# Batch 0 of a windowed attention with a squared-ReLU layer behind it: begun in two groups of 256 tokens, with a smaller masking bias and a new order of the first steps

## The chip, the core and the metric

One core of a Trainium2 chip runs the whole kernel. It has five engines with instruction streams of their own: TensorE (PE, with its weight loads as PEld), VectorE (DVE), ScalarE (ACT), GpSimd (POOL) and SyncE (SP); SP, ACT and POOL issue DMAs, each on a queue of its own. The metric is the device time of one execution in microseconds (us), as the median of several.

## The reference

Attention with four sink tokens and a window of 128, then a two-layer network with a squared ReLU on the result:

```
scores = q @ k.T / sqrt(64);  keep = (key < 4) | (0 <= query - key < 128)
x = (softmax(where(keep, scores, -1e9)) @ v)   # 4 batches, 8 heads, 768 tokens, 64 wide
x = x.transpose(0, 2, 1, 3).reshape(3072, 512)
out = relu(x @ w_in) ** 2 @ w_out              # w_in 512 x 2048, w_out 2048 x 512
```

## The kernel before

All work is cut into numbered steps (`op`, on about 990 places), each for one engine. A table, `ORDER`, lists the steps in the order in which they are recorded, with a letter for the engine that takes the step (p PE, d DVE, a ACT, g POOL) and the choice of a bank; each engine executes its own steps in that order and waits by semaphores for what they need. `DUMMIES` says how many dummy matmuls PE executes ahead of a step (`warm`, line 185, and the warm-up of line 1368, which works on `tri`).

A batch of 768 tokens goes through attention in blocks of 256 tokens (s = 0, 1, 2), and through layer 1 (with w_in) and layer 2 (with w_out) in pieces. For batch 0 the start is this:

- **Loads.** SP loads q and k of the first 512 tokens in fp32 into `qr` (line 351), a pair of heads at a time, 256 KB each, four tokens side by side in a partition. POOL's queue loads v (line 381), w_in in four quarters (line 308), then q and k of the last 256 tokens and of later batches, cast to bf16 on the way (`qn`, line 372), and w_out (line 316). ACT's queue loads four rows of v per head (`vs_in`, line 424), which POOL spreads into `vs` (line 554, "vs products").
- **Transposes.** A cast (line 194 on DVE, 192 on ACT) regroups `qr` into bf16 `qs`; PE transposes it into PSUM (`pt`, line 507); an unload copies it to `qkT` (lines 194, 192).
- **Attention of a block.** Scores of a head pair go to PSUM (`ps`, line 613). In block 0 the mask is added on PE ahead of them, as two matmuls of the identity with `sg`, which holds the bias (line 606). ACT takes the exponential (line 634) into `expm`; in blocks 1 and 2 a mask follows on DVE (line 646) or POOL (line 218). PE multiplies with v (`po`, line 682, "values"); DVE takes a reciprocal and normalizes (lines 698 and 699, "norm") into `xn_sb`. PE transposes that (`px`, line 731, "bridge"), and a copy (line 194 or 192) puts it into `xT`.
- **Layer 1.** A piece is 16 matmuls of 256 columns, a quarter of w_in with a block of 256 tokens (`pm`, line 763); DVE or ACT takes the ReLU and the square. A quarter of w_in has to have landed.

Batch 0 is read in groups of tokens, 512 and 256:

```
GROUPS[0] = [(0, 4), (512, 2)]          # first token, number of blocks of 128
for m in range(NP):                      # NP = 4 pairs of heads
    for ti in (1, 0):                    # k, then q
        load_qk(0, m, ti, 0, 1)
```

The four pairs of heads of the first group come one after the other: cast k, cast q, four transposes each, two unloads, then the pair's scores. The bias is built on POOL (`build_bias`): two selects over four blocks of 128 columns, a copy of them to a second half, and there a memset of the four sink rows.

## Time and profile before

| what | value |
|---|---|
| median of 3 runs | 209.63 us (209.41 to 209.71) |
| the profiled execution: span from its first to its last instruction | 208.6 us |
| PE busy in it | 199.8 us (96%) |
| DVE, ACT, POOL busy | 178.4, 133.0, 98.2 us |
| DMA, software queue (POOL's) | 12.59 MB, 79.6% of 16 engines' span |
| DMA, hardware queue (SP's) | 13.01 MB, 27.0% |

The profile gives no time for the profiled execution other than its span; the runs' median lies 1.0 us above it. In a row of a timeline stand the start in us, the duration in us, the engine, the line of the code, the operation and its tiles, and how many instructions the row merges; in brackets the idle time before the first of them and what ended it. Matmuls are pipelined, so that the starts of a row's neighbours say how long it keeps PE; its duration holds the last matmul's way through the array. In a table of windows each engine has its busy us, with the number of instructions in parentheses; DMA share is the mean over 16 engines and can be above 1 where packets overlap. SPq, ACTq and POOLq are DMA issues.

### The profile page before, as it was taken

What the parts mean: (1) busy time and instruction counts of PE and PEld (TensorE: products, weight loads), DVE (VectorE), ACT (ScalarE), POOL (GpSimd) and SP (SyncE); (2) the same over time, 40 slices, a digit from 0 to 9 for tenths busy, and PEclk for the clock granted to TensorE, in tenths of its full rate; (3) what the DMA queues carried; (4) which work ended last, traced back from release to release, by engine and by line L of the source; (5) the groups of instructions that cost most, each with busy time, mean ns of one, the idle gap of its engine ahead of it and who ended that gap; (6) DMA issues with size and microseconds to landing.
All of it is one profiled execution on the core that took longest, in us unless ns stands there. A gap on an engine that the chain in (4) does not pass through costs nothing.

```text
span 208.6 us, 6015 instructions
## 1 busy us (share of the span) xinstructions
PE 199.8 (96%) x2498; PEld 176.1 (84%) x2500; DVE 178.4 (86%) x342; ACT 133.0 (64%) x208; POOL 98.2 (47%) x138
## 2 busy tenths in 40 slices
PE   7789899999899999999999999999999999999993
PEld 7548796679778889989878988998889999999893
DVE  5757566996989998999998788999989998998853
ACT  2595728548988168899888448989871452584110
POOL 7988164999489936999423628000280000000000
PEclk9999999999999999999999999999999999999999
DMA  5999999999989999999998996901023220200205
GB/s 150 280 185 204 178 193 214 170 155 188 121 55 135 146 142 210 126 167 155 140 149 216 95 129 172 155 3 25 3 50 123 57 80 24 104 0 0 100 4 201
DMA packets 93994, 26.10 MB, mean 125 GB/s; under 512 B 86800, under 2 KB 91408, under 8 KB 93968
## 3 DMA queue, kind: packets, MB, share of 16 engines
q0 software_dynamic: 69248, 12.59, 79.6%
q1 hardware_dynamic: 24536, 13.01, 27.0%
q8 instruction: 19, 0.31, 0.6%
q10 hardware_dynamic: 184, 0.14, 0.2%
q14 instruction: 7, 0.06, 0.1%
HBM read 27.30 MB, written 6.29 MB: 161 GB/s over the span
## 4 chain that ended last, share of the span: by engine, by line
PE 65%; POOL 12%; DVE 9%; DMA 6%; ACT 3%; issue 2%; POOLq 0%; ACTq 0%
PE py L1238 25%; PE pm L891 25%; DMA w_in_sb<-in_moe_w_in_dram 6%; PE pm L763 4%; PE ps L613 4%; POOL v L381 3%; PE po L682 3%; POOL qn L372 3%; POOL vs L554 2%; PE py L1099 2%; ACT expm L634 1%; POOL expm L218 1%; PE pt L507 1%; DVE sg L1212 1%; POOL w_in_sb L308 1%
## 5 line engine op out<-in xcount | busy, mean ns | idle before, releaser
L634 ACT ACTIVATE expm<-ps 128x1024 bf16<-128x1024 f32 (+1 forms) x48 | 43.9, 951 | 9.4 <-PE ps L613 7.5
L218 POOL TENSOR_SCALAR_AFFINE_SELECT expm<-expm 128x512 bf16<-128x512 bf16 x34 | 25.4, 782 | 43.8 <-DVE xn_sb L699 19.5
L941 DVE CUSTOM_DVE_ANT_0 r<-pm,t 128x512 bf16<-128x512 f32 x54 | 36.1, 685 | 1.6 <-PE pm L891 1.1
L1238 PEld LDWEIGHTS <-gT_sb 128*128 128x128 bf16 x320 | 30.4, 98 | 4.5 <-issue 0.8
L891 PEld LDWEIGHTS <-w_in_sb 128*128 128x128 bf16 x384 | 32.4, 114 | 1.7 <-issue 1.5
L192 ACT ACTIVATE t<-pm 128x512 f32<-128x512 f32 x42 | 24.7, 600 | 13.5 <-PE pm L891 12.7
L891 PEld LDWEIGHTS <-wi 128*128 128x128 bf16 x288 | 24.7, 114 | 0.8 <-issue 0.7
L1238 PEld LDWEIGHTS <-sg 128*128 128x128 bf16 x240 | 22.4, 98 | 3.2 <-DVE sg L1212 0.3
L192 ACT ACTIVATE osb<-py 128x256 f32<-128x256 f32 (+1 forms) x36 | 14.1, 398 | 15.7 <-PE py L1238 15.0
L763 PE MATMUL pm<-xT,w_in_sb 128*128 128x256 bf16 x192 | 22.5, 273 | 1.0 <-DMA w_in_sb<-in_moe_w_in_dram 1.0
L763 PEld LDWEIGHTS <-w_in_sb 128*128 128x128 bf16 x192 | 20.5, 114 | 1.9 <-DMA w_in_sb<-in_moe_w_in_dram 1.2
L891 PE MATMUL pm<-xs,wi 128*128 128x256 bf16 (+1 forms) x192 | 21.6, 246 | 0.0
L891 PE MATMUL pm<-xs,w_in_sb 128*128 128x256 bf16 (+1 forms) x192 | 21.5, 246 | 0.0
L1238 PE MATMUL py<-wt,gT_sb 128*128 128x256 bf16 x160 | 20.7, 273 | 0.2
L1238 PE MATMUL py<-wt,sg 128*128 128x256 bf16 x160 | 20.8, 273 | 0.0
L1238 PE MATMUL py<-w_out_sb,gT_sb 128*128 128x256 bf16 x160 | 20.4, 273 | 0.0
L914 ACT ACTIVATE gT_sb<-r 128x1024 bf16<-128x1024 bf16 x17 | 18.0, 1056 | 1.8 <-DVE r L941 1.6
L682 PE MATMUL po<-v,expm 128*128 128x65 bf16 x352 | 17.9, 193 | 0.3 <-ACT expm L634 0.3
L682 PEld LDWEIGHTS <-expm 128*128 128x128 bf16 x352 | 16.7, 97 | 1.7 <-ACT expm L634 0.5
L699 DVE TENSOR_TENSOR xn_sb<-po,rc 128x512 bf16<-128x512 f32 (+1 forms) x28 | 17.2, 615 | 1.0
L1252 DVE TENSOR_TENSOR osb<-py,osb 128x256 f32<-128x256 f32 x30 | 12.1, 418 | 4.7 <-PE py L1238 4.6
L613 PE MATMUL ps<-qkT 64*128 64x128 bf16 (+1 forms) x256 | 14.3, 238 | 0.8 <-ACT expm L634 0.6
(109 smaller groups left out, 383.3 us busy)
## 6 DMA issues: line engine op xcount, KB each, us to landing
out_dram<-osb SPq DMA_DIRECT2D x11, 512.0 KB, 4.9
v<-in_v_dram POOLq DMA_DIRECT2D x24, 128.0 KB, 6.8
qn<-in_k_dram POOLq DMA_DIRECT2D x20, 128.0 KB, 6.5
qn<-in_q_dram POOLq DMA_DIRECT2D x20, 128.0 KB, 6.4
w_in_sb<-in_moe_w_in_dram POOLq DMA_DIRECT2D x4, 512.0 KB, 10.5
w_out_sb<-in_moe_w_out_dram POOLq DMA_DIRECT2D x4, 512.0 KB, 10.9
qr<-in_k_dram SPq DMA_DIRECT2D x4, 256.0 KB, 5.6
qr<-in_q_dram SPq DMA_DIRECT2D x4, 256.0 KB, 5.2
```

Of the source, the lines that this page charges most:

```text
L192: return nc.scalar.activation(out=dst, in_=src, func=AF.Copy)
L218: nc.gpsimd.affine_select(out=e_tile, in_=e_tile, compare_op=ALU.is_ge, fill=fill, base=i - 1, pattern=[[0, n], [1 if i else -1, 128]], ch ...
L613: nc.tensor.matmul(ps[:, h2, o:o + w], lhsT=qkT_sb[r, m, 1, c, :], rhs=qkT_sb[r, m, 0, qb:qb + w // 128, :], start=(i == 0 and not biased) ...
L634: nc.scalar.activation(out=x[:, :, o:512], in_=bank_t["s", b, s, m][:, :, o:512], func=AF.Exp, scale=scale)
L682: touch(("po", b, s, m0), e, nc.tensor.matmul(pv[:, i, h2, :], lhsT=lhsT, rhs=rhs, start=(n_ == 0), stop=(n_ == len(mms) - 1)), j)
L699: touch(("po", b, s, m0), e, nc.vector.tensor_tensor(out=xn_sb[:, 2 * s:2 * s + 2, 128 * (m0 + j0):128 * (m0 + j0 + nj)].rearrange("p i (j ...
L763: nc.tensor.matmul(pm[:, i, :], lhsT=w_in_sb[:, fb // 4, kb, fb % 4:512:4], rhs=xT[:, c0 // 256:(c0 + cw) // 256, kb, :], start=(kb == 0), ...
L891: touch(tag, e, nc.tensor.matmul(y[:, bk, i, :], lhsT=weights(name, f0 + i, a), rhs=rhs[:, a, :], start=fresh and i == 0 and a == 0, stop= ...
L914: nc.scalar.activation(out=d, in_=x, func=AF.Square)
L941: touch(tag, e, nc.vector._custom_dve(TENSOR_ADD_SAT, out=d.rearrange("p n c -> p (n c)"), in0=T["y"][:, 1].rearrange("p n c -> p (n c)"), ...
L1238: touch((b, u), e, nc.tensor.matmul(region(name), lhsT=x[:, i, :], rhs=w_[:, i, :], start=first and i == 0, stop=i == HB - 1, skip_group_c ...
L1252: ins = nc.vector.tensor_tensor(out=d, in0=region(of), in1=d, op=ALU.add)
```

## The change

- Batch 0 is read in three groups of 256 tokens. In the first two, q and k are loaded two tokens side by side, two pairs of heads at a time: eight loads of 256 KB as before, in rows of 512 bytes instead of 1024. The two q loads of the first group go from SP's queue to ACT's, and `vs_in` of batch 0 from ACT's to SP's, behind the first two k loads.
- A transposing step then holds two pairs of heads (8 transposes: k and q, two blocks of 128 tokens), and an unload one pair's k and q. The numbers of casts, transposes, unloads and score matmuls stay.
- The bias has three blocks of 128 columns: a select over two, a select over one, the memset of the sink rows. POOL's copy goes.
- The memsets of batch 0's v, kblk and vs come ahead of the other fills, and v's comes first.
- Layer-1 steps of batch 0's first two blocks are cut in halves of 8 matmuls, so that other steps can stand between.
- `ORDER` is new for the first 185 steps; behind them it is the old one with four added to each number. `DUMMIES` had 60 matmuls on 7 steps and has 95 on 6.

Two places show it, in the order of the instructions on an engine. The first is the start of POOL's stream: bias (`sg`), v, w_in, head rows and vs products. Before:

```order
L244 AFFINE_SELECT ident_165<-ident_165 128x128
L218 AFFINE_SELECT sg_168<-sg_168 128x2x128 x2
L254 COPY sg_168<-sg_168 128x512
L255 MEMSET sg_168 4x256
L381 DMA v0_181<-in_v_dram 128x8x64 x2
L308 DMA w_in_sb_170<-in_moe_w_in_dram 128x4x512
L264 AFFINE_SELECT head_rows_169<-head_rows_169 32x8
L267 AFFINE_SELECT head_rows_169<-head_rows_169 32x8
L554 TENSOR_TENSOR vs0_174<-vs_in_178,head_rows_169 32x130 x4
L381 DMA v0_181<-in_v_dram 128x8x64 x2
L308 DMA w_in_sb_170<-in_moe_w_in_dram 128x4x512 x3
```

and now:

```order
L244 AFFINE_SELECT ident_165<-ident_165 128x128
L380 DMA v0_181<-in_v_dram 128x8x64 x2
L218 AFFINE_SELECT sg_168<-sg_168 128x2x128
L218 AFFINE_SELECT sg_168<-sg_168 128x128
L254 MEMSET sg_168 4x256
L263 AFFINE_SELECT head_rows_169<-head_rows_169 32x8
L266 AFFINE_SELECT head_rows_169<-head_rows_169 32x8
L218 AFFINE_SELECT tri_166<-tri_166 128x128 x2
L550 TENSOR_TENSOR vs0_174<-vs_in_178,head_rows_169 32x130 x4
L307 DMA w_in_sb_170<-in_moe_w_in_dram 128x4x512
L380 DMA v0_181<-in_v_dram 128x8x64 x2
L307 DMA w_in_sb_170<-in_moe_w_in_dram 128x4x512 x3
```

The first two v loads move ahead of the bias, and the first quarter of w_in behind the vs products. The second place is DVE between the scores of block 0 and the first layer-1 piece: unloads of transposes (`qkT<-pt`), norms of four head pairs (`rc`, `xn_sb`) and the copies of the bridge (`xT<-px`, the last row in the second listing). Before, all unloads stand ahead of the norms:

```order
L194 COPY qkT0_179<-pt_349 128x512 x2
L194 COPY qkT0_179<-pt_372 128x512
L698 RECIPROCAL rc_446<-po_406 128x4
L699 TENSOR_TENSOR xn_sb_183<-po_406,rc_446 128x2x128
L698 RECIPROCAL rc_449<-po_406 128x4
L699 TENSOR_TENSOR xn_sb_183<-po_406,rc_449 128x2x128
L698 RECIPROCAL rc_452<-po_428 128x4
L699 TENSOR_TENSOR xn_sb_183<-po_428,rc_452 128x2x128
L698 RECIPROCAL rc_455<-po_428 128x4
L699 TENSOR_TENSOR xn_sb_183<-po_428,rc_455 128x2x128
```

and now (`po_395` holds pairs 0 and 1, `po_423` pairs 2 and 3; `pt_412` and `pt_466` are the second group's transposes):

```order
L694 RECIPROCAL rc_430<-po_395 128x4
L695 TENSOR_TENSOR xn_sb_183<-po_395,rc_430 128x2x128
L694 RECIPROCAL rc_441<-po_395 128x4
L695 TENSOR_TENSOR xn_sb_183<-po_395,rc_441 128x2x128
L194 COPY qkT0_179<-pt_412 128x2x256
L694 RECIPROCAL rc_458<-po_423 128x4
L695 TENSOR_TENSOR xn_sb_183<-po_423,rc_458 128x2x128
L694 RECIPROCAL rc_463<-po_423 128x4
L695 TENSOR_TENSOR xn_sb_183<-po_423,rc_463 128x2x128
L194 COPY qkT0_179<-pt_466 128x2x256 x2
L194 COPY xT0_184<-px_444 128x512 x2
```

Three unloads of the second group stand between and behind the norms. The diff, with the table cut to its first lines:

```diff
 ORDER = """
-986 0 1 2 7 8 9 10 11 12 13 14 15 16 17 18 987+0 3 5 19 20 21 6 79 22 23 24 25 55d 56d 57+0 58 59 60a 83+0 85 103+1
...
+990 1 0 2 7 8 9 10 11 12 13 14 15 16 17 18 56a 991+0 55d 61a 3 60d 57+1 62+0 19 20 59a 5 6 58d 4 65 63d 67+0 21 64a
...
 """
 DUMMIES = {
-    987: 29, 58: 8, 63: 10, 64: 4, 83: 3, 91: 3, 97: 3,
+    57: 31, 62: 24, 75: 4, 85: 3, 110: 4, 991: 29,
 }
 
 
@@ -155,8 +156,7 @@
     ident = consts.tile([128, 128], BF16)
     tri = consts.tile([128, 2, 128], BF16)
     mask0 = consts.tile([128, 1, 3, 128], BF16)
-    biases = rooms["sg"][0].tile([128, 8, 128], BF16, name="sg", tag="sg0")
-    bias, bias0 = biases[:, 0:4, :], biases[:, 4:8, :]
+    bias = rooms["sg"][0].tile([128, 3, 128], BF16, name="sg", tag="sg0")
     head_rows = consts.tile([32, H, 1], BF16)
     w_in_sb = consts.tile([128, 4, NKB, 512], BF16)
     w_out_sb = consts.tile([128, NFB, DM], BF16)
@@ -230,9 +230,9 @@
         nc.vector.memset(vs_in[:, :, D:D + 1], 1.0)
 
     def fill_one(i):
+        nc.vector.memset(v_sb[i][:, :, :, D:D + 1], 1.0)
         nc.vector.memset(kblk[i], 0.0)
         nc.vector.memset(vs_sb[i], 0.0)
-        nc.vector.memset(v_sb[i][:, :, :, D:D + 1], 1.0)
 
     def fill_first(e):
         fill_one(0)
@@ -249,10 +249,9 @@
             triangles(tri[:, i:i + 1, :], i, 1)
 
     def build_bias(e):
-        for i in range(2):
-            triangles(bias.rearrange("p (j i) c -> p i j c", i=2)[:, i], i, 2, -30000.0)
-        nc.gpsimd.tensor_copy(out=bias0, in_=bias)
-        nc.gpsimd.memset(bias0[0:NSINK, 1:3, :], 0.0)
+        triangles(bias[:, 0:3:2, :], 1, 2, -30000.0)
+        triangles(bias[:, 1:2, :], 0, 1, -30000.0)
+        nc.gpsimd.memset(bias[0:NSINK, 0:2, :], 0.0)
 
     def build_masks(e):
         nc.gpsimd.tensor_copy(out=mask0[:, 0, 0:1, :], in_=tri[:, 1:2, :])
@@ -270,7 +269,7 @@
 
     bias_slot = Slot("sg", 4)
     c_const = op(-9, {"dve": 0.85}, fill, takes=[bias_slot])
-    c_fill = op(-8.9, {"dve": 0.95}, fill_first, after=[c_const])
+    c_fill = op(-8.9, {"dve": 0.95}, fill_first)
     c_rest = op(-0.3, {"dve": 0.95}, fill_second, after=[c_const])
     c_ident = op(-9, {"pool": 0.3}, build_ident, after=[c_const])
     c_tri = op(-0.15, {"pool": 0.6}, build_triangles, after=[c_const])
@@ -326,7 +325,7 @@
 
 
     GROUPS = {b: [(0, 6)] for b in range(B)}
-    GROUPS[0] = [(0, 4), (512, 2)]
+    GROUPS[0] = [(0, 2), (256, 2), (512, 2)]
     GROUPS[1] = [(0, 4), (512, 2)]
     ROW = {512: 0.03, 1024: 0.052}
 
@@ -348,11 +347,11 @@
             qr_t[b, "all", m0, ti, g] = t
             for m in range(m0, m0 + pairs):
                 qr_t[b, m, ti, g] = t[:, 2 * (m - m0):2 * (m - m0) + 2, :]
-            return [nc.sync.dma_start(
+            return [(nc.sync if ti or g else nc.scalar).dma_start(
                 out=t,
                 in_=(q, k)[ti][b, 2 * m0:2 * m0 + 2 * pairs, t0:t0 + 128 * n, :].rearrange(
                     "h (p t) d -> p h (t d)", t=n))]
-        o = dma_op("sp", ("qk", b, m0, ti, g), run, 16 * pairs * ROW[256 * n] + (0.7 if (b, m0, ti, g) == (0, 0, 0, 0) else 0.0), behind,
+        o = dma_op("sp" if ti or g else "act", ("qk", b, m0, ti, g), run, 16 * pairs * ROW[256 * n] + (0.7 if (b, m0, ti, g) == (0, 0, 0, 0) else 0.0), behind,
                    () if half else [qr_slot[share]], yields)
         for m in range(m0, m0 + pairs):
             ops["qk", b, m, ti, g] = o
@@ -466,21 +465,18 @@
                             ops["turn", b, ti, t].margin = 5.167
                             copies.append(ops["turn", b, ti, t])
                     ops["cast", b, s] = ops["v", b, 2 * s + 1]
-            w = 2 if n == 2 and t0 else 1
+            w = 2 if n == 2 else 1
             for m in range(0, NP, w) if b not in NATURAL else ():
                 f = 0.08 * m
                 bs = Slot(side, 2)
                 regs = []
-                casted = (b, g) != (0, 0)
+                casted = b > 0 or g == 2
                 for ti in () if casted else (1, 0):
                     sl = qs_slot[b, m, ti, g] = Slot("qs", 1)
 
                     def regroup(e, m=m, ti=ti):
-                        t = qs_t[b, m, ti, g] = bank(qs_slot[b, m, ti, g], "qs", [128, w, n, 2, D], BF16)
-                        if w == 2:
-                            copy(e, t, qr_t[b, "all", m, ti, g].rearrange("p (m h) (t d) -> p m t h d", m=2, d=D))
-                        else:
-                            copy(e, t[:, 0], qr_t[b, m, ti, g].rearrange("p h (t d) -> p t h d", d=D))
+                        t = qs_t[b, m, ti, g] = bank(qs_slot[b, m, ti, g], "qs", [128, n, 2 * w, D], BF16)
+                        copy(e, t, qr_t[b, "all", m, ti, g].rearrange("p h (t d) -> p t h d", d=D))
                     who = {"pool": 0.17 + w * n * 0.125}
                     who["dve"] = 0.06 + w * n * (0.094 if b else 0.115)
                     if w == 1:
@@ -507,7 +503,7 @@
                                     touch(("pt", b, m, g), e, nc.tensor.matmul(
                                         pt[:, h, o + 128 * t:o + 128 * t + 128],
                                         lhsT=qn_t[b, ti][:, t0 // 128 + t, 128 * (m + j):128 * (m + j) + 128]
-                                        if casted else qs[ti][:, j, t, :, :], rhs=ident, is_transpose=True,
+                                        if casted else qs[ti][:, t, 2 * j:2 * j + 2, :], rhs=ident, is_transpose=True,
                                         start=(t == 0 and (w == 1 or ti == 1)),
                                         stop=(t == n - 1 and (w == 1 or ti == 0))), h)
                     tr = op(at(f + 0.03), {"pe": 0.02 + 0.055 * n * w * len(part)}, transpose,
@@ -605,7 +601,7 @@
                                 for h2 in range(2):
                                     nc.tensor.matmul(
                                         ps[:, h2, o:512], lhsT=ident,
-                                        rhs=(bias if s else bias0).rearrange("p j c -> p (j c)")[:, o:512],
+                                        rhs=bias.rearrange("p j c -> p (j c)"),
                                         start=True, stop=False)
                             for i, (o, c, qb, w) in enumerate(segs):
                                 for h2 in range(2):
@@ -756,14 +752,19 @@
         bs, rs = Slot(("den", "att"), 1), Slot("r", 1)
         tag = (b, fbs[0], c0)
 
-        def mm(e):
-            pm = bank_t[tag] = bank(bs, "pm", [128, n, cw], FP32)
-            for i, fb in enumerate(fbs):
+        def mm(e, part):
+            if not part[0]:
+                bank_t[tag] = bank(bs, "pm", [128, n, cw], FP32)
+            pm = bank_t[tag]
+            for i in part:
+                fb = fbs[i]
                 for kb in range(NKB):
                     nc.tensor.matmul(pm[:, i, :], lhsT=w_in_sb[:, fb // 4, kb, fb % 4:512:4],
                                      rhs=xT[:, c0 // 256:(c0 + cw) // 256, kb, :], start=(kb == 0), stop=(kb == NKB - 1))
-        a = op(key, {"pe": n * NKB * cw / 2350.0}, mm, takes=[bs],
-               after=[o for s in need for o in ops["xT", b, s]] + [w_in_op[fbs[0] // 4]])
+        a = None
+        for part in (range(0, 2), range(2, 4)) if b == 0 and c0 < 512 else (range(n),):
+            a = op(key, {"pe": len(part) * NKB * cw / 2350.0}, lambda e, part=part: mm(e, part), takes=[] if a else [bs],
+                   after=[o for s in need for o in ops["xT", b, s]] + [w_in_op[fbs[0] // 4]], follow=[a] if a else [])
         ops["layer1", b, fbs[0], c0] = a
         first_layer1.setdefault(b, a)
 
@@ -1285,13 +1286,15 @@
     NATURAL, TURNED, BIASED = (2, 3), (), 1
     FAST = {1: ((0, 1), (2,)), 2: ((0,), (1, 2)), 3: ((0,), (1, 2))}
     CLASSIC2 = ((0, 0),)
-    load_sinks("act", 0)
-    for m in range(NP):
-        for ti in (1, 0):
-            load_qk(0, m, ti, 0, 1)
+    for g in range(2):
+        for m in (0, 2):
+            for ti in (1, 0):
+                load_qk(0, m, ti, g)
+            if m and not g:
+                load_sinks("sp", 0)
     for b in range(1, B):
         load_sinks("sp", b)
-    load_v(0, 0, None, [("qk", 0, 3, 0, 0)])
+    load_v(0, 0, None, [("qk", 0, 2, 0, 1)])
     load_w_in(0)
     load_v(0, 1)
     for i in range(1, 4):
@@ -1314,7 +1317,8 @@
             at = attention(0, lambda f: f - 1.0)
             at(0, 0.0, 1.0, ("den", "att"))
             late["masks"] = op(0.006, {"pool": 1.0}, build_masks, after=[c_tri, ops["bridge", 0, 0]])
-            at(1, 0.2, 0.725, ("att", "den"))
+            at(1, 0.0, 1.0, ("den", "att"))
+            at(2, 0.2, 0.725, ("att", "den"))
         done = FAST.get(b, ())
         if b == 0:
             for i in range(4):
```

71 lines of the change are left out of this document (36 added, 35 removed).

## The prediction

> **What bounds the kernel now.** I read the table of windows first, for where TensorE (PE) is not busy, then its waits, then the chain that ended last.
>
> ```profile
> core 0: us, PE busy (x) PEld busy (x) DVE busy (x) ACT busy (x) POOL busy (x), PEclk, DMA share, GB/s
> 0.00:17.13 17.13, 13.82 (x176) 10.34 (x177) 11.27 (x31) 10.78 (x17) 14.31 (x29) 1.00 1.22 204
> 17.13:30.00 12.87, 11.87 (x149) 11.66 (x146) 8.33 (x16) 6.00 (x8) 6.87 (x11) 1.00 1.70 189
> 45.00:208.60 163.60, 159.26 (x2012) 143.52 (x2010) 146.22 (x278) 107.95 (x174) 65.12 (x88) 1.00 0.96 106
> ```
>
> From 45 us on PE is busy for 159.26 of 163.60 us. It loses 3.3 us before 17.13 and 1.0 us in the next window. So an early microsecond comes through to the end, if PE meets no new wait. Its waits, all kinds, over the whole run:
>
> ```profile
> engine line waited for: us in total, times, longest us
> PE pw L1368 <- DVE tri L224: 1.3, 1, 1.3
> PE pm L763 <- DMA w_in_sb<-in_moe_w_in_dram: 1.0, 1, 1.0
> PE pt L507 <- DVE qs L194: 0.9, 2, 0.6
> PE ps L613 <- ACT expm L634: 0.6, 1, 0.6
> PE pt L507 <- ACT qs L192: 0.6, 2, 0.4
> ```
>
> The largest that can go is the second: layer 1 of batch 0 waits for the last quarter of w_in. The chain of waits shows when that quarter lands, and what PE does then:
>
> ```profile
> 11.95 13.55 DMA w_in_sb<-in_moe_w_in_dram
> 25.51 0.05 issue
> 25.55 5.43 PE pm L763 x48
> ```
>
> So PE stands ready at 24.5 us and goes on at 25.55. What counts is when the new order comes to the same instruction, and how much it has done by then.
>
> **The change part by part.** *What stands ahead of the last quarter.* Before, three layer-1 pieces of 16 matmuls are done when PE reaches it; in the new order it is three pieces and two half pieces, 16 matmuls more. A piece:
>
> ```profile
> 22.19 1.91 PE L763 MATMUL pm<-xT,w_in_sb 128*128 128x256 bf16 x16
> 23.94 0.61 PE L731 MATMUL px<-ident,xn_sb 128*128 128x128 bf16 x8
> ```
>
> 22.19 to 23.94 is 1.75 us. Break-even is therefore 25.55 + 1.75 = 27.3 us: the kernel gains what the new order comes earlier than that. I now add up its way there.
>
> *To the second set of transposes.* PE first runs 29 and then 31 dummies (29 and 8 before).
>
> ```profile
> 1.27 3.27 PE L1368 MATMUL pw<-tri 128*128 128x128 bf16 x29 [1.27 <-DVE tri L224]
> 4.77 1.06 PE L185 MATMUL pt<-ident 128*128 128x128 bf16 x8
> 6.45 0.40 PE L507 MATMUL pt<-ident,qs 128*128 128x128 bf16 x4 [0.63 <-DVE qs L194]
> 8.03 0.73 PE L185 MATMUL pt<-ident 128*128 128x128 bf16 x10
> ```
>
> By starts and counts a dummy takes 0.107 us in the first two rows and 0.056 in the last, so the clock rose between 5.6 and 6.45 us; I take 6.3. From 1.27 to 6.3 that is 47 dummies, and 13 more take 0.7: the first 8 transposes start at 7.0 and end at 7.5. Then come 24 dummies (1.35) and 8 transposes (0.45): 9.3 us. If the clock rose right behind the first 29 dummies, the other 31 would end at 6.1, and at 7.7 if it rose behind them all: bounds of -0.9 and +0.7. The Trainium skill ("TensorE: Matmul & The Clock Gate", "What's actually happening") says that the clock rises after a busy window of some 3.4 us that runs free of the kernel's start. The trace agrees as far as one rise can, some 5 us behind the first matmul; by that rule the place could be another in each run, and the transposes could start at an estimated 6.2 to 7.7 us.
>
> Is the data there? Two casts show when loads arrived, and one row how long ACT's queue took over its first issue:
>
> ```profile
> 0.82 1.30 ACTq L424 DMA_DIRECT2D vs_in<-in_v_dram  x1
> 5.78 0.62 DVE L194 CAST qs<-qr 128x512 bf16<-128x512 f32 x1 [1.75 <-DMA qr<-in_q_dram]
> 7.50 2.35 DVE L194 CAST qs<-qr 128x512 bf16<-128x512 f32 x4 [0.51 <-DMA qr<-in_q_dram]
> q1 hardware_dynamic: 24536, 13.01, 27.0%
> ```
>
> Two of the 256 KB loads are in at 5.78, four at 7.50, and the new loads have that size, in rows of 512 B instead of 1 KB. ACT now issues the two q loads of the first group; at 1.30 us each they and its table load (1.28) are over by 4.7, ahead of any data. If rows cost nothing, the second pair is in at 7.5, cast at 8.1, and hidden behind the dummies that end at 8.85. Nearest for a short row is the mean of the hardware queue, whose row gives packets, MB and the share of 16 engines' span: 13.01 MB in 24536 packets is 530 B, and 27.0% of 16 engines' 208.6 us is 37 ns for each. At 50 ns for 1 KB (some 310 a us on 16 engines) two short rows cost 1.4 times a long one; the second pair then lands at 9.1 and is cast at 9.75. I take the lower end, as the queue's other packets are transposes and stores; 0 and 0.9 us stay as bounds. The Trainium skill ("DMA: Bandwidth & Descriptors", "Specifications") gives 512 B as the least transfer at line rate; by it the cost would be nothing, by the row up to 0.9 us.
>
> *To the first layer-1 matmul.* Four score blocks follow, each 2 bias and 4 score matmuls, in the order of head pairs 0, 2, 3, 1; pair 1 is last, and everything behind hangs on its exponential.
>
> ```profile
> 13.48 0.49 PE L606 MATMUL ps<-sg,ident 128*128 128x384 bf16 x2
> 13.91 0.34 PE L613 MATMUL ps<-qkT 64*128 64x256 bf16 x4
> 14.18 0.54 PE L682 MATMUL po<-v,expm 128*128 128x65 bf16 x12
> L634 ACT ACTIVATE expm<-ps 128x768 bf16<-128x768 f32 x3 | 2.4, 804 | 0.1
> 13.29 0.35 PE L682 MATMUL po<-v,expm 128*128 128x65 bf16 x6
> 13.68 0.18 DVE L698 RECIPROCAL rc<-po 128x4 f32<-128x4 f32 x1 [0.58 <-PE po L682]
> ```
>
> A block took 0.70 us here, 0.1 of it a gap ahead of the score matmuls that I expect to close when blocks follow each other: 0.6 (0.70 stays as bound). Four blocks and 4 dummies: 9.3 + 2.6 = 11.9. Exponential 0.8 with 0.1 ahead of it: 12.8. Values to reciprocal 0.4: 13.2.
>
> From here VectorE (DVE) sets the pace. It does the last three of four norms with the norm of pair 1 first, three unloads of the second group's transposes between them, and two copies of xT last; before, the unloads were all over by then.
>
> ```profile
> 15.13 0.17 DVE L698 RECIPROCAL rc<-po 128x4 f32<-128x4 f32 x1
> 15.68 0.17 DVE L698 RECIPROCAL rc<-po 128x4 f32<-128x4 f32 x1
> 9.76 1.27 DVE L194 COPY qkT<-pt 128x512 bf16<-128x512 bf16 x2
> 16.26 0.86 DVE L194 COPY xT<-px 128x512 bf16<-128x512 bf16 x2
> ```
>
> Norms 3 x 0.55, unloads 3 x 0.63, copies 0.86: 4.4 us. The first layer-1 matmul starts at 13.2 + 4.4 = 17.6 us (17.13 before). The scores, exponentials and transposes that PE and ACT do meanwhile fit beside it; PE idles there.
>
> *From there to the last quarter.* Three pieces of 16 and two halves (4 x 1.75), one score block without bias (0.35, as 16.58 to 16.91 below), four value blocks of 0.4 and a bridge of 0.45: 9.4 us. Arrival 17.6 + 9.4 = 27.0.
>
> ```profile
> 16.58 0.39 PE L613 MATMUL ps<-qkT 64*128 64x128 bf16 x6
> 16.91 0.29 PE L572 MATMUL pk<-qkT,kblk 128*32 128x256 bf16 x4
> 18.91 0.23 PE L682 MATMUL po<-v,expm 128*128 128x65 bf16 x2
> 19.32 1.94 PE L763 MATMUL pm<-xT,w_in_sb 128*128 128x256 bf16 x16
> ```
>
> Of the value blocks (18.91 to 19.32 is one), three now wait for masks on POOL instead of one:
>
> ```profile
> 17.09 1.23 POOL L218 TENSOR_SCALAR_AFFINE_SELECT expm<-expm 128x512 bf16<-128x512 bf16 x2
> 6.77 1.95 POOL L554 TENSOR_TENSOR vs<-vs_in,head_rows 32x130 bf16<-32x130 f32 x4
> 8.67 1.83 POOL L381 DMA_DIRECT2D v<-in_v_dram  x2
> ```
>
> Three masks of 1.23 run beside 3 us of layer-1 pieces; I count 0, and 0.3 as bound. On POOL's queue the first w_in quarter moves behind the four vs products (1.95), and the products behind vs_in, which now rides SP behind two loads. So that quarter is issued some 3 to 4 us later; the v loads ahead of it go out 1.7 us sooner. All w_in issues are out by about 14 us (12.7 before), and that queue carries the same bytes, so I keep 25.5 us for the last landing, with 1.5 us to spare; gone, each further microsecond would count in full. The bias in three steps saves POOL a copy and a select, hidden by the loads; splitting layer 1 in halves costs no matmul; the smaller memsets lie ahead of the first cast.
>
> *Sum.* 27.3 - 27.0 = 0.3 us off the profiled span of 208.6: 208.3. The median of the runs shown, 209.63, lies 1.0 us above that span, for what is ahead of the first and behind the last instruction; so **209.3**. With the bounds (blocks +0.4, loads +0.9, masks +0.3; clock -0.9 to +0.7) it goes from 208.4 to 211.6, all at once.
>
> **The rivals.**
> 1. *The DVE row starts late (slower).* Place: the second transposes and the four blocks behind them. If the second pair lands at 9.1 and blocks take 0.70, the first layer-1 matmul starts at 18.9 and the loss is 1.0: 210.6; with half of it, 210.0. It decides as soon as that matmul starts after 27.3 - 9.4 = 17.9 us. For it: only 0.3 us separates my sum from that, and DVE has no hole in the row. Against: the 24 dummies cover loads up to 8.85.
> 2. *An earlier start (much faster).* If the clock rises right behind the first 29 dummies, the first layer-1 matmul comes at 16.7 and the arrival at 26.1; norms and unloads that overlap more than the rows show would add to it. The floor is the landing at 25.5: a gain of 1.2 to 1.8, so 207.8 to 208.4. For it: from 5.6 to 6.45 us PE was mostly idle, so the trace doesn't show what fixes the place. Against: data arrives no sooner than 5.78 + 0.62. The free-running window of the Trainium skill's page would allow it in some runs.
> 3. *It does not do what it says.* First scores come no earlier, since 55 dummies stand ahead of them and the loads share the same 16 engines; the waits that go are paid back in DVE's row, and the last quarter slips to 27 us: 209.6.
>
> **How the numbers follow.** A measurement of this kernel can tell about 0.2%, 0.4 us, from no change. My forecast, 208.8 to 209.6 as its own range, has 0.46 (0.26 of it beyond 0.2%, 0.20 within). Rival 1 has 0.30 (0.28 slower, 0.02 within), rival 2 has 0.18 (faster), rival 3 has 0.06 (within). Faster 0.44, same 0.28, slower 0.28. The range 208.2 to 210.6 leaves out the far ends of rivals 1 and 2.
>
> **What would show it.** Right: first scores at 9 to 10 us, the exponential of the last pair ending near 12.8, DVE without a hole from 13.2 to 17.6, first layer-1 matmul before 17.9, and no wait of PE for w_in. Wrong: transposes that wait for a cast after their dummies, a layer-1 start after 18, or a wait for w_in that stays, which would mean that the loads, not PE and DVE, set the early part. A new PE wait after 45 us would take back what was won.

## The result, and the profile after

The changed kernel is slower: 210.73 us as the median of 20 executions (209.94 to 211.79), beside 209.76 us for the kernel before (20 executions, 209.2 to 210.9). The ratio is 1.0036, as that of the means (210.65 and 209.88), with a 95% interval of 1.0021 to 1.005; the medians lie 0.97 us apart. A second measurement (e2 below) gave 1.0034, 1.0009 to 1.0058. 209.3 us was forecast, with a range up to 210.6.

The profiled execution does not look like that. It took 209.94 us, the least of its 20, with a span of 208.2. The table of windows of the changed kernel, as it was read for the kernel before:

```profile
core 0: us, PE busy (x) PEld busy (x) DVE busy (x) ACT busy (x) POOL busy (x), PEclk, DMA share, GB/s
0.00:17.13 17.13, 14.52 (x205) 11.76 (x206) 10.71 (x31) 9.26 (x15) 11.99 (x26) 1.00 1.25 198
17.13:30.00 12.87, 12.52 (x159) 12.16 (x156) 7.40 (x15) 7.50 (x9) 11.30 (x17) 1.00 1.71 188
45.00:208.20 163.20, 158.89 (x2011) 143.41 (x2008) 147.41 (x279) 106.08 (x171) 65.01 (x88) 1.00 1.03 107
```

PE is busy for 0.7 us more in each of the first two windows, and loses 4.3 us behind 45 us, as before. Its waits, the longest first (line 503 is the transposes, 609 the scores, 762 layer 1):

```profile
engine line waited for: us in total, times, longest us
PE pw L1372 <- DVE tri L224: 1.3, 1, 1.3
PE pt L503 <- ACT qkT L192: 0.6, 1, 0.6
PE ps L609 <- ACT expm L630: 0.6, 1, 0.6
PE pm L762 <- DVE xT L194: 0.4, 1, 0.4
```

The wait for the last quarter of w_in is gone. The chain of waits shows what sets the first layer-1 matmul in this execution (its rows of `issue` and ACTq are left out):

```profile
0.82 4.11 DMA qr<-in_q_dram
4.95 8.88 DMA qr<-in_q_dram
13.91 0.63 ACT qs L192
14.54 0.50 ACT qkT L192
15.07 0.40 PE pt L503 x4
15.49 1.29 DVE qkT L194 x2
16.78 0.67 DVE xT L194 x2
17.50 1.03 PE pm L762 x8
```

SP issues the last q load of the second group at 4.95, as soon as the first q load has landed, and it lands at 13.8; ACT has waited for it. Layer 1 starts at 17.50 (17.6 forecast). The bridge ends at 23.34, and 32 matmuls later (2 x 1.75 us) PE is at the last quarter, at 26.84 (27.0 forecast). By these two profiles alone the change gains what was forecast: 208.6 to 208.2. The measured times say the opposite, so the question is what a usual execution of each kernel looks like. In each execution of the changed kernel the time lies 1.7 to 1.8 us above the span (209.94 and 208.2, 211.79 and 210.0).

### The profile page after: what moved, and what is told of

The parts are those of the page before. It is cut to its first block, busy times and chain, and to the rows that moved or that the text cites. A ratio compares the mean times of both kernels' runs of the same rounds, so it can differ in the third digit from the quotient of the medians.

```text
span 208.2 us, 6087 instructions
## 1 busy us (share of the span) xinstructions
PE 200.9 (96%) x2535; PEld 177.6 (85%) x2535; DVE 178.0 (85%) x343; ACT 131.6 (63%) x205; POOL 98.6 (47%) x141
## 4 chain that ended last, share of the span: by engine, by line
PE 76%; DVE 10%; DMA 6%; ACT 5%; issue 1%; ACTq 0%
PE py L1239 25%; PE pm L892 25%; PE pm L762 9%; DMA qr<-in_q_dram 6%; PE po L678 5%; PE ps L609 4%; PE py L990 3%; PE py L1100 2%; PE pt L503 1%; DVE sg L1213 1%; DVE xn_sb L695 1%; DVE r L942 1%; ACT gT_sb L915 1%; ACT qkT L192 1%; DVE gT_sb L1213 1%
## 5 line engine op out<-in xcount | busy, mean ns | idle before, releaser
L218 POOL TENSOR_SCALAR_AFFINE_SELECT expm<-expm 128x512 bf16<-128x512 bf16 x38 | 26.5, 730 | 46.9 <-ACT expm L630 21.5
```

The source lines that it names most:

```text
L218: nc.gpsimd.affine_select(out=e_tile, in_=e_tile, compare_op=ALU.is_ge, fill=fill, base=i - 1, pattern=[[0, n], [1 if i else -1, 128]], ch ...
```

## What a usual execution of the kernel before does

**e1_before, e9_before_look, e10_before_look: the kernel before, with no edit.**

> The unchanged kernel of before, against itself. It tells how far a profile's span stands below its execution's time, and where a median execution of before lies. Theory A (the clock: the start of the changed kernel is paced by dummy matmuls on PE and so hangs on where its clock rises) and theory B (the loads: the last q load of the second group, landed at 13.82 us in the changed kernel, sets the start) both expect that the time lies some 1.7 us above the span, as in the changed kernel's runs, so that the profile of 208.6 us belonged to an execution of about 210.3 us, and a median one has a span near 208.1. If time less span is 1.0 here, the conversion of the prediction was right and the whole miss lies in the changed kernel. Ratio 1.000 within 0.2%.

> The kernel before, one more profile of its start. Theory E (the bound: the 25.55 us at which TensorE went on after its wait for w_in belonged to one slow execution; a typical one gets there at about 24.9 us, with a wait of 0.3 us or none, as in e5): TensorE reaches the last quarter at 24.7 to 25.1 us and the span is 207.8 to 208.2. If the wait of 1.0 us is there again with a span near 208.3, the prediction's break-even of 27.3 us was typical and the loss lies elsewhere.

> The same, a further profile: theory E as in e9, 24.7 to 25.1 us; the other theory 25.5 us after a wait of about 1 us. Over all profiles of before, the span should follow that time: span less 183.0 us.

The ratio of e1 was 1.0002 (0.9974 to 1.0029), and its profiled execution took 211.01 us with a span of 209.3. So 1.7 us lie between the two here as well, and the profile that the prediction read, span 208.6, belongs to an execution of about 210.3 us, 0.6 above the median. The rows in which PE reaches the last quarter of w_in, in e9 and then in e10:

```profile
24.83 2.37 PE L763 MATMUL pm<-xT,w_in_sb 128*128 128x256 bf16 x20 [0.70 <-DMA w_in_sb<-in_moe_w_in_dram]
```

```profile
25.39 1.83 PE L763 MATMUL pm<-xT,w_in_sb 128*128 128x256 bf16 x15 [0.62 <-DMA w_in_sb<-in_moe_w_in_dram]
```

| profile | layer 1 starts | at last quarter | its wait for w_in | span | time |
|---|---|---|---|---|---|
| before | 17.13 | 25.55 | 1.0 | 208.6 | |
| e1 | 18.73 | 26.14 | under 0.1 | 209.3 | 211.01 |
| e9 | 16.75 | 24.83 | 0.7 | 208.1 | 209.79 |
| e10 | 17.38 | 25.39 | 0.6 | 208.5 | 210.22 |
| e5 (below) | 16.92 | 24.94 | under 0.1 | 208.1 | 209.79 |

The span is that time plus 183.0 to 183.3 us in all five. The median of 209.76 us (span 208.05) then stands for a last quarter at 24.9 us, and the highest of the medians measured later, 210.17, for 25.3. The wait for w_in stands in three of the five, so it was nothing odd. In e1 and e5 it is too short for the list: there the bridge's start and the next matmul lie 0.50 and 0.52 us apart, where 0.45 is usual, and the last quarter lands at 26.1 and 24.9. So the landing sets the arrival in all five, and it moves between 24.8 and 26.1 us from one execution to the next; 25.55 is late. e9 came as theory E had it, but for the length of the wait; e10 is nearer to the other theory (25.5 us). E holds for the median, whose 24.9 to 25.3 us are worked back from times and spans, not for every execution, and not in that the wait would be missing.

e1 is a case of its own: DVE waited 3.1 us for a load of q, PE 2.45 us for the cast behind it, and the granted clock (PEclk) reads 0.76 from 8 to 14 us, 1.00 in the same window of the other four.

## What a usual execution of the changed kernel does

**e2_after, e11_after_look, e13_after_look, e14_after_look, e15_after_look: the changed kernel, with no edit.**

> The changed kernel unchanged, for a second profile, if possible of an execution nearer to the median (span 209.0) than the first (208.2). Theory A: the clock rises later than 4.56 us in it (6 us or later), the first 8 transposes end after 6.9 us instead of 6.8 and the first layer-1 matmul starts about 0.5 to 1 us later than 17.5, in step with the span. Theory B: the last q load lands later than 13.82 us and the first layer-1 matmul follows it at 3.7 us, wherever the clock rises. If the first layer-1 matmul starts at 17.5 and the span is still near 209, the loss lies behind the start (rival C). Time 210.7, ratio 1.004 to 1.005.

> The changed kernel, one more profile. Theory E: the first layer-1 matmul at 17.5 to 17.7 us and the arrival at the last quarter at 26.9 to 27.1 us, as the prediction had it, 0.3 to 0.4 us worse than a typical execution of before (24.9 + 1.75 = 26.65 us); the span 208.3 to 208.5 plus what TensorE waits for the transposing DMA near 130 us.

> The changed kernel, one more profile, to meet an execution near its median span of 209.0 us (so far 208.2, 208.3, and 209.7 with a late wait of 1.2 us). Theory K (the clock rises at another place in each execution; as late as 7.7 us the 60 dummies end at 7.7 instead of 7.0 and all behind them moves with it): where the span is 208.8 to 209.2 without a late wait, the clock rises behind 6.5 us and the first layer-1 matmul starts at 18.0 to 18.4 us. Theory D2 (late waits are more common than the looks showed): layer 1 starts at 17.5 to 17.7 us and a wait of 0.3 to 0.8 us for the transposing DMA stands near 130 us. Theory L (loads): layer 1 starts late behind a q, k or v load that lands late.

> The same, a further profile; the expectations of theories K, D2 and L are those of e13: K a rise of the clock behind 6.5 us with layer 1 at 18.0 to 18.4 us, D2 a wait near 130 us with layer 1 at 17.5 to 17.7 us, L a late load ahead of a late layer 1.

> The same, a further profile, with the expectations of e13: K a rise of the clock behind 6.5 us with layer 1 at 18.0 to 18.4 us, D2 a wait near 130 us with layer 1 at 17.5 to 17.7 us, L a late load ahead of a late layer 1.

Six profiles of the changed kernel, and two of e6, which has the same start. Times in us; "last q cast" is ACT's cast of the second group's last q load, with * where ACT waited for the load:

| profile | 2nd transposes start | last q cast | layer 1 starts | late wait | span | time |
|---|---|---|---|---|---|---|
| after | 7.97 | 13.91* | 17.50 | | 208.2 | 209.94 |
| e2 | 8.63 | 13.60 | 17.71 | 1.2 | 209.7 | 211.49 |
| e11 | 8.10 | 13.98* | 17.57 | | 208.3 | 210.03 |
| e13 | 8.18 | 14.24* | 17.83 | 0.3 | 209.2 | 210.94 |
| e14 | 8.40 | 13.37 | 17.48 | 1.4 | 209.7 | 211.37 |
| e15 | 8.86 | 13.83 | 17.94 | | 208.7 | 210.44 |
| e6 | 8.60 | 13.57 | 17.68 | | 208.5 | 210.29 |
| e16 (as e6) | 9.27 | 14.25 | 18.36 | | 209.4 | 211.20 |

Theories A (the clock) and B (the last q load) both miss on e2: it starts layer 1 close to the first profile (17.71), and its extra time is the late wait behind 45 us (rival C). e11 came as expected.

Two things can set the start of layer 1. In the five profiles without * it comes 9.08 to 9.09 us behind the second transposes, which end PE's row of 60 + 24 dummies: the chain that the prediction summed. The chain of waits of e15 has it from dummies (line 185) to transposes (503), bias matmuls (602), the exponential of pair 1, values (678) and DVE's row of norms (695), unloads (`qkT`) and copies (`xT`); rows of `issue`, of the scores (609) and of the reciprocals (694) are left out, and `...` stands for the first two blocks with the dummies between them:

```profile
4.55 2.69 PE pt L185 x31
7.23 0.45 PE pt L503 x8
7.68 1.34 PE pt L185 x24
9.02 0.45 PE pt L503 x8
...
10.99 0.43 PE ps L602 x2
11.69 0.43 PE ps L602 x2
12.44 0.82 ACT expm L630
13.30 0.37 PE po L678 x6
13.91 0.42 DVE xn_sb L695
14.34 0.60 DVE qkT L194
15.06 0.43 DVE xn_sb L695
15.60 0.42 DVE xn_sb L695
16.03 1.20 DVE qkT L194 x2
17.22 0.67 DVE xT L194 x2
17.94 1.04 PE pm L762 x8
```

In the three with * the clock had risen earliest, and the last q load landed 8.9 to 9.1 us after its issue, in the other five 7.4 to 7.5; why the two go together is open. Layer 1 follows that cast at 3.59 us. What moves the second transposes is the clock of PE. The timeline of the first execution and that of e16, first row of dummies and first transposes:

```profile
4.34 2.01 PE L185 MATMUL pt<-ident 128*128 128x128 bf16 x31
6.18 0.61 PE L503 MATMUL pt<-ident,qs 128*128 128x128 bf16 x8
```

```profile
4.34 3.31 PE L185 MATMUL pt<-ident 128*128 128x128 bf16 x31
7.49 0.61 PE L503 MATMUL pt<-ident,qs 128*128 128x128 bf16 x8
```

31 dummies take 1.84 us here and 3.15 us there. At 0.056 and 0.107 us each, the clock rose at about 4.6 and at 7.3 us. (It is the spacing that shows this; PEclk reads 1.00 from 0 to 8 us in both.) So the rise moves the start as theory K has it, at the late end; at the early end the last q load takes over.

The late wait is a third term, theory D2. In e2, e13 and e14, PE waits near 130 us for a transposing DMA of batch 3's q. e13 is theory L (a late load) with some of D2, e14 is D2 with a wait longer than expected, e15 and e16 are K (e15 at 17.94, just short of its 18.0; the span of e16, 209.4, is above its 209.1). The chain of e14:

```profile
126.49 0.04 issue
126.53 4.59 DMA qkT<-qn
131.12 0.14 issue
131.26 0.40 PE pk L568 x4
```

Without it, the span is the start of layer 1 plus 190.7 to 191.1 us in all eight. The starts of the six have a mean of 17.67 us and the late waits one of 0.47 us (2.83 in six): 190.8 + 17.67 + 0.47 is 208.9, the median span of the 20 executions is 209.0, so the usual execution is accounted for within 0.1 us. Counted from the last quarter, the span is 181.4 to 181.7 us more than the arrival in all eight, 183.0 to 183.3 in the kernel before: the 16 matmuls that the changed kernel has ahead are worth what the prediction gave them (1.75).

## Is the late wait what the change costs?

**e5_before_turn_first, e6_after_turn_first, e16_after_turn_first_look.** One swap in the order table of both kernels lets SP issue that transposing DMA ahead of one of `xn_sb` (in e16 the kernel of e6 once more):

```diff
-... 712 521 713 ...      (before)
+... 712 713 521 ...
-... 716 525 717 ...      (after)
+... 716 717 525 ...
```

> The kernel before, with one swap far behind the change: the last transposing DMA of batch 3's q (issued at 126.33 us there) goes ahead of the last one of xn. TensorE's sink scores of batch 3 (pk, near 130 us) need it; in e2 they waited 1.2 us for it, in the two profiles of before not at all (1.4 and 0.7 us to spare). Theory D (late wait: part of the changed kernel's loss is this wait, which strikes in some executions only): the transfer lands 1.2 us earlier, and the time falls only as far as the kernel before has such executions, 0 to 0.2 us: ratio 0.999 to 1.000. Theory S (all of the loss is at the start): no change, 1.000.

> The changed kernel with the same swap. Theory D: the wait of 1.2 us goes, the tail of the executions above 209.5 us of span with it, and the mean falls by 0.3 to 0.5 us: 210.2 us, ratio 1.001 to 1.002. Theory S: ratio stays at 1.0035, and a profile shows a layer-1 start later than 17.7 us where the span is 209 or more.

> The kernel of e6 (the changed kernel with the transposing DMA of batch 3's q ahead), one more profile, so that the late wait is out of the way. Theory K: span 208.2 to 209.1, in step with the place where the clock rises (4.5 to 7.7 us). Theory D2: span 208.2 to 208.5 with layer 1 at 17.5 to 17.7 us. Theory L: a late load ahead of a late layer 1.

Ratios to the kernel before: e5 0.9989 (0.9964 to 1.0013), e6 1.0025 (1.0003 to 1.0046). No late wait is left in the profiles of e6 and e16. The changed kernel falls by 0.001 (1.0034 to 1.0025), and so does the one before (1.0002 to 0.9989): the distance between the two stays, so nothing here makes theory D (the late wait) the cause of the difference, though intervals of 0.2% each way leave room for a part of it; 1.0025 lies between what D (1.001 to 1.002) and S (1.0035) had for e6. Theory S, that the loss lies at the start, has the two profiles for it (span 208.5 with layer 1 at 17.68, 209.4 with 18.36). The late wait costs both something, if anything. In the five profiles of the kernel before with the old order (e8, below, among them) this DMA landed 2.4 us after its issue; in three of six of the changed one it took 4.2 to 4.6. That may be chance; it is left open.

## Do the dummies cost what they take?

**e3_fewer_dummies and e7_after_turn_first_fewer_dummies** (the second with the swap of e6):

```diff
-    57: 31, 62: 24, 75: 4, 85: 3, 110: 4, 991: 29,
+    57: 12, 62: 12, 75: 4, 85: 3, 110: 4, 991: 29,
```

> The changed kernel with 12 dummies in place of 31 ahead of the first transposes and 12 in place of 24 ahead of the second. Theory A: 31 dummies fewer take 1.7 us (warm) to 3.3 us (cold) from PE's own row ahead of the scores, so casts set that part; the first layer-1 matmul comes 0.5 to 1 us earlier in a median execution, 210.0 us; unless the clock then rises later and the score blocks run at half speed, which would show as 0.107 us matmul spacing. Theory B: scores come earlier, but the second group's transposes still wait for the last q load: first layer-1 matmul still near 17.5 us, time 210.7 within 0.3.

> The changed kernel with that swap and 12 + 12 dummies in place of 31 + 24. Theory D: e3's start was 0.3 to 0.5 us earlier than the changed kernel's (layer 1 at 17.18 us), and its long tail (spans up to 210.6) was the late wait; without that the time is 209.6 to 209.9, ratio 0.997 to 0.999. Theory S: the tail stays, as it comes from the wait of the values for v (0.8 us in e3), and the ratio stays near 1.003.

e3 1.0032 (1.0006 to 1.0059), e7 1.0013 (0.9988 to 1.0039). The second transposes start at 7.6 us and layer 1 at 17.18 and 17.00, some 0.6 us earlier than the changed kernel's mean, but a new wait takes part of the gain. In the timeline of e7 the values of block 0 meet it:

```profile
11.89 0.46 PE L678 MATMUL po<-v,expm 128*128 128x65 bf16 x10 [0.68 <-DMA v<-in_v_dram]
```

So the dummies do hold the start, and they hide that v is late. The time follows less than theory A had it (210.0): e3 shows no gain that can be told from none; e7 takes half of the loss away, but its interval overlaps that of e6, and 1.0013 is neither what theory D (0.997 to 0.999) nor what S (1.003) had.

**e12_v_ahead_fewer_dummies**: e7 with the two v loads ahead of the identity's select on POOL.

```diff
-... 61a 3 60d 57+1 62+0 19 20 59a ...
+... 61a 19 20 3 60d 57+1 62+0 59a ...
```

> e7 (the changed kernel with 12 + 12 dummies and the swap of the transposing DMA) with the first two v loads issued ahead of the identity's select on POOL, near 1.6 us instead of 1.89. In e7 the values of block 0 waited 0.7 us for v. Theory E (the changed start has two costs, dummies that cover no load and the v that they hide): v lands about 0.3 us earlier, the layer-1 start moves from 17.0 to 16.7 us, the arrival at the last quarter to 26.1 us, and the ratio to before falls from 1.0013 to about 1.000. If the start hangs on another load (the last q load of the second group, landed at 12.56 us in e7), nothing moves: ratio 1.0013.

1.0013 (0.9979 to 1.0047), and a miss: POOL's row for these loads starts at 1.89 us as before, because it waits for DVE's memset of v, not for the identity.

```profile
1.89 1.90 POOL L380 DMA_DIRECT2D v<-in_v_dram  x2 [1.36 <-DVE v L233]
```

## What do the loads do to each other?

**e4_v_later**: the changed kernel, with the first two v loads behind the bias.

```diff
-... 62+0 19 20 59a 5 6 58d 4 65 63d ...
+... 62+0 59a 5 6 58d 4 19 20 65 63d ...
```

> The changed kernel with the first two v loads issued on POOL behind bias, head rows and triangles (as late as in the kernel before) instead of ahead of them. Theory B: the software queue then starts moving near 9 us instead of 5.9, the last q load of the second group lands near 12 instead of 13.82 us, and the first layer-1 matmul comes up to 1 us earlier unless the values of block 0 wait for v: 209.9 to 210.3. Theory A: the first layer-1 matmul doesn't move and the time stays at 210.7 or rises by a wait of the values for v.

1.0136 (1.0105 to 1.0166), the largest effect of all. Theory B is right on the loads: the last q load of the second group lands 5.5 us after its issue (7.4 to 9.1 in the changed kernel), near 10.5 us, and the last two casts need not wait. Its time holds only where the values don't wait for v; they wait 1.9 us, as theory A's second half had it, and layer 1 starts at 18.90. That is not the price of a late v alone: behind this wait PEclk reads 0.72 from 14 to 20 us (1.00 in the changed kernel). The windows tell how the loads share the 16 engines: q and k in rows of 1 KB (before and e9, 5 to 7 us), in rows of 512 B by themselves (e4), and with v's queue beside them (after):

```profile
5.00:7.00 2.00, 1.37 (x16) 1.06 (x15) 1.21 (x2) 0.11 (x1) 1.85 (x5) 1.00 0.99 319
5.00:7.00 2.00, 1.84 (x19) 1.55 (x19) 0.86 (x2) 0.60 (x1) 1.85 (x5) 1.00 1.07 365
```

```profile
6.50:8.80 2.30, 2.30 (x41) 1.96 (x38) 1.14 (x3) 1.69 (x3) 2.04 (x5) 1.00 1.18 290
```

```profile
6.50:9.50 3.00, 3.00 (x49) 2.47 (x47) 1.45 (x3) 2.00 (x4) 2.07 (x5) 1.00 1.49 210
```

319 and 365, 290, and 210 GB/s. The shorter rows cost a tenth to a fifth, the v loads beside them more.

**e8_before_v_first**: the kernel before, with the v loads ahead of the bias.

```diff
-986 ... 987+0 3 5 19 20 21 6 79 ...
+986 ... 987+0 3 19 20 5 21 6 79 ...
```

> The kernel before with one part of the change alone: the first two v loads ahead of the bias on POOL, issued near 1.9 us instead of 3.45. Theory B (loads share the engines: the group loads of q and k slow down as soon as the queue of v moves): the last q and k casts come 1 to 2 us later than 11.2 us and the first layer-1 matmul at 18 to 19 us; as far as TensorE is then still ahead of the last w_in quarter (it waited 1.0 us for it), the time stays: 0 to +0.8 us, ratio 1.000 to 1.004. If the loads don't share, the casts stay within 0.3 us and the ratio is 1.000.

1.0015 (0.9987 to 1.0042), layer 1 at 17.10: nothing moved. It doesn't test what it should: POOL issues v only at 3.04 us (3.45 before), again behind the memsets. That the change puts v's memset first is what lets v go at 1.88.

**e17_group2_later and e18_group2_later_no_gap_dummies**: e7 with three small loads of later batches ahead of the second group's four; e18 also without the dummies of step 75.

```diff
             if m and not g:
-                load_sinks("sp", 0)
-    for b in range(1, B):
-        load_sinks("sp", b)
+                for b in range(B):
+                    load_sinks("sp", b)
```

```diff
-    57: 12, 62: 12, 75: 4, 85: 3, 110: 4, 991: 29,
+    57: 12, 62: 12, 85: 3, 110: 4, 991: 29,
```

> e7 (12 + 12 dummies, the transposing DMA ahead) with the three vs_in loads of later batches issued by SP ahead of the second group's four loads of q and k instead of behind them. Those four are then issued about 2 us later, and the two v loads, which wait for no one, get more of the 16 engines. Theory E2 (with the dummies gone the start hangs on v at 11.85 us, which shares the engines with the second group): v lands 0.5 to 1.5 us earlier, the wait of the values for v (0.7 us) goes, the first layer-1 matmul starts at 16.4 to 16.8 us instead of 17.0 and the ratio falls below 1.000 (e7: 1.0013). Rival: the second group then lands later than 13 us and its cast, transposes and unload end the DVE row later: layer 1 at 17.5 us or later, ratio above 1.002.

> e17 without the four dummies between the first and the second score block. Theory E2: the score blocks end 0.23 us earlier, and as far as the values don't wait for v, layer 1 starts up to 0.23 us earlier than in e17; ratio 0.001 below that of e17. If v or the second group's loads bind, layer 1 starts where it does in e17 and the ratio is the same within 0.0005.

e17 0.9999 (0.9975 to 1.0022), e18 0.9983 (0.997 to 0.9997). The first two v loads, least, median and most from issue to landing, in e7 and in e17:

```profile
DMA to landing us min/median/max: 7.1/8.0/8.9
```

```profile
DMA to landing us min/median/max: 6.3/6.3/6.4
```

Their issues start at 1.89 and 2.94 in both, so the second lands near 9.2 us instead of 11.85, and the wait for v is gone. The last q load of the second group loses little by it; ACT casts it at 12.82 us (12.64 in e7). But layer 1 starts at 17.09, no earlier than in e7. The chain of e17 shows what is late next: the second group's first q load, which lands at 10.91 us (DVE casts it at 10.11 in e7) and whose cast DVE has to make ahead of the norms.

```profile
5.80 5.11 DMA qr<-in_q_dram
10.91 0.02 issue
10.93 0.93 DVE qs L194 x2
```

So theory E2 is right on v and wrong on the start. The rival is right on where it then hangs, DVE's row, but not on its sizes (17.5 us or later, above 1.002). The profiled execution of e18 (210.06 us) is the slowest of its 11, median 209.38; its layer 1 starts at 17.32, later than in e17, so the profile doesn't show where the lower time comes from. e18 is 0.17% below the kernel before and some 0.5% below the changed one (0.9983 to 1.0036). Against the kernel before that is only just outside the interval, and it is the best of several versions measured; a repeat would have to confirm it.

## Why the prediction was wrong, step by step

1. **Break-even at 27.3 us: this step failed.** It took the 25.55 us at which PE went on after its wait for w_in from one execution. A median one gets there at 24.9 to 25.3 us, so break-even is at 26.65 to 27.05, and an arrival at 27.04 gains nothing or loses up to 0.4. The landing "at 25.5 us" is a spread of 24.8 to 26.1. The other term, 1.75 us for 16 matmuls, held.
2. **Arrival at 27.0: right, in part by luck.** The six profiles give 26.84 to 27.3, mean 27.04. Inside the sum two errors cancel. Blocks took 0.70 us and not 0.6 (10.99 to 11.69 in e15), 0.4 in all; the second transposes ended at 8.4 to 9.3 us in the six, where 9.3 was forecast, as the clock mostly rose earlier than 6.3. DVE's row lasted 4.3 (13.67, the end of the values, to 17.94 in e15; 4.4 forecast). The prediction's bounds for the clock (6.1 to 7.7 for the end of 60 dummies) held all eight profiles, 6.2 to 7.5. The Trainium skill ("TensorE: Matmul & The Clock Gate", "What's actually happening") has the clock's window run free of the kernel's start; the eight places, 4.6 to 7.3 us, agree in that they differ.
3. **The 24 dummies "cover loads up to 8.85": they do, and no load needs that.** The changed kernel's row of the second pair's last cast on ACT shows how early it has its load:

```profile
6.83 0.63 ACT L192 ACTIVATE qs<-qr 128x512 bf16<-128x512 f32 x1 [1.25 <-DMA qr<-in_q_dram]
```

   It is over at 7.5 us, the dummies at 8.0 to 9.3; with fewer of them the transposes start at 7.6. So these dummies hold PE 0.5 to 1.8 us longer than the data does. The 512-B rows cost the first group nothing, as taken. The Trainium skill ("DMA: Bandwidth & Descriptors", "Specifications") gives 512 B as the least transfer at line rate; the rows of 512 B here moved 290 GB/s by themselves, those of 1 KB 319 and 365. What the sum left out is the second group: its last q load lands near 12.5 or near 14 us (the last q and k of that part by 11.3 before) and takes back an early rise of the clock. Rival 2, which priced that rise at 16.7, came in no profile, though the clock did its part in the first: by PE's row alone layer 1 would have started there at 7.97 + 9.08 = 17.05, and the load made it 17.50.
4. **No wait of PE for w_in: right** in every profile of the changed kernel; the last quarter lands at 25.1 to 25.6 in the six (25.5 forecast).
5. **No new wait behind 45 us: wrong in three of six profiles.** The prediction named such a wait as what would take back the gain. Its mean is 0.47 us in the six; by the swap it is 0.2 us (1.0034 to 1.0025, inside the intervals), and the kernel before gains as much by that, so its part in the difference is between nothing and 0.47.
6. **The 1.0 us from span to time: wrong**, it is about 1.7 in each execution of both kernels. The error has the same root as step 1: the one profile of before was read as a median execution.

Together, against the forecast gain of 0.3 us: 0.25 to 0.65 by step 1, 0.04 by step 2, 0 to 0.47 by step 5, so anything from level to a loss of 0.9 us. Measured are 0.75 (0.4 to 1.05 by the interval), or 0.97 by the medians; step 1 alone brings the gain of 0.3 to nothing or turns its sign, and the sizes are not settled closer than that. Of the absolute miss of 1.4 us, step 6 is 0.7; the other 0.7 is span (208.3 forecast, 209.0 measured), most of it the late waits of step 5. Step 1 is not in it, since 25.55 and 208.6 come from the same execution: it accounts for the sign of the change, not for the time. Rival 1 has the sign and nearly the size (210.0 to 210.6), but of its mechanism only the blocks of 0.70, not the second pair landing at 9.1: layer 1 starts behind its point of 17.9 us in one of six profiles only; that point, worked back from 27.3, was itself 0.25 to 0.65 us too late.

What stays open: how often the late wait strikes each kernel, why the transposing DMA takes 2.4 us in some executions and over 4 in others, and how the loss divides between start and late wait. e6 bears on the last: its twelve executions have a mean span of 208.8, and 208.8 less 181.4 would be an arrival of 27.4 if nothing waits late in them, so the usual start may be worse than in the six profiles.

## What to carry to other kernels

Ahead of a forecast below one per cent, profile the same kernel several times, and take the time and the span of the same execution: a wait on the last of a queue of transfers ends at another time in each, and a break-even read from one profile can be off by more than the gain. Dummies that keep the clock up belong where data isn't there yet; where they stand ahead of work whose data has come, the start hangs on when the clock rises. When transfers with different due times share the engines, holding the later ones back lets the earlier land sooner; look at each of the held ones, though. In e17 the last of them was done at about the same time, but the first came 0.8 us later and then set the start.

## What the runs showed of the hardware that was not expected

- The place where PE's clock rises, as matmuls of 128 columns go from 0.107 to 0.056 us, moves by 2.7 us between executions with the same start (4.6 to 7.3 us from the span's start in eight profiles), and with it every instruction that PE alone paces.
- Behind long waits of PE the granted clock was lower in two executions: PEclk reads 0.76 from 8 to 14 us in e1, which has a wait of 2.45 us, and 0.72 from 14 to 20 us in e4, behind two waits of 1.9 us together. With the wait of 1.06 us in e10 it stays at 1.00.
- Two v loads whose packets go out beside those of four loads of q and k landed 7.1 and 8.9 us after their issue; with the four held back by 2.6 to 3.4 us, 6.3 and 6.4. The last of the four was cast at 12.82 instead of 12.64, the first q of them 0.8 us later.
- The same load of 256 KB, issued at 4.9 to 5.1 us, landed near 12.5 us in some executions and near 14 in others (8.88 us in the first profile's chain).
- The same transposing DMA took 2.4 us from issue to landing (the kernel before, issued at 126.33) or 4.59 us (e14).
